# Hash attention and two feed-forward layers: the weight conversions and the sums of layer two rank 100 instructions later

## The chip, the cores and the metric

The kernel runs on one core of a Trainium2 chip. The metric is the device time of one execution in microseconds; the time shown is the median of three runs. TensorE (PE) multiplies matrices and loads weights (PEld) beside that; VectorE (DVE), ScalarE (ACT) and GpSimd (POOL) work element by element; SyncE (SP) issues nearly all DMAs, in the order of its queue.

## The reference

```python
# attention: q, k, v of 2 batches x 8 heads x 768 positions x 64
q_bits = einsum(q, proj) > 0;  k_bits = einsum(k, proj) > 0      # 6 bits each
mask   = q_bucket[..., :, None] == k_bucket[..., None, :]
scores = where(mask, q @ k.T / 8, -1e9)
attn   = exp(scores - max) / (sum + 1e-9);   out = attn @ v
# layer one: x is 1536 x 512, w_in 512 x 2048, w_out 2048 x 512
h = maximum(x @ w_in, 0);                    x = (h * h) @ w_out
# layer two: the same sizes
h = x @ w_in;  g = maximum(h, 0) + alpha * minimum(h, 0);  y = g @ w_out
```

The arrays of both layers come as float64, laid out by the host; the kernel gets them as their bits, two 32-bit words for each number.

## The kernel before, in words

The 1536 tokens are four chunks of 384. The attention of the first chunk runs alone (`attention_first`, L529). Then follow four passes of layer one, one for each chunk (`feed_forward`, L813); beside the passes of chunks 0 to 2 the attention of the next chunk is woven in, as a list of small steps (`attention_beside`, L572). The pass of the last chunk turns the result for layer two. Layer two takes two chunks at a time (`wide_hidden`, L989, and `whole_project`, L1075); its first product runs by a scheme with seven products in place of eight, for which sums of weight blocks are made beforehand.

All products are made of two parts of each operand: a rounded high part and the rest, and three matmuls (high by high, high by low, low by high). For a block of 128 hidden rows `split` (L737) makes the high part on ACT (L713) and the rest on VectorE or POOL (L714); `hidden` (L742) runs 12 matmuls with it (L752 to L754), and `project` (L786) runs those of the second product (L793, L794, L797).

Converting weights. `load_bits` (L648) loads 128 x 512 numbers of 8 bytes into one of three buffers `wbits`. `to_f32` (L654) makes float32 of them: ACT scales the upper words into `we` (L661), VectorE keeps the sign in `wsg` (L663), merges the bits of the lower words (L664), and joins both (L669). `we` and `wsg` have one buffer each. Layer one's 32 blocks are converted in `fetch` (L726) during the pass of chunk 0, two blocks of hidden rows ahead of their use, and stored to DRAM (L735); later passes load them from there (L731). Layer two's 32 blocks are converted during the passes of chunks 1 and 2: 16 of the second matrix in `ahead` (L672, stored at L676), 16 of the first in `sums_ahead` (L682), where VectorE then makes four sums of each pair of blocks (L697 to L700) and SP stores the results (L702, L703). These steps are spread over the passes from 1.0 to 2.9 by a list with marks:

```python
conversion = Background(steps, [(1.0, 0), (NCH - 1.1, len(steps))])
```

The attention beside: for each pair of heads and block of 128 queries, `scores` (L420) runs four matmuls (L426), VectorE takes the row maximum `low` (L434), and ACT the exponential `sm` (L435); `p_t` (L442) transposes it on TensorE (L451), and VectorE (L458) or ACT (L456) copies it to `pt`; `av` (L472) multiplies by the values. Hash bits (L254, L258), matches (L276, L302) and reciprocals of the sums (L483 to L488) come between.

The order on the engines. The program is traced instruction by instruction, and each gets a rank, its place in the trace. When the program is built, a scheduler goes through a model of the engines: an engine that is free takes, of its instructions that are ready, the one of lowest rank. The order that results is fixed for each engine and queue, and on the chip every engine works through its list in order. `tc.high_priority(offset=n)` takes n off the ranks of the instructions traced inside it. Before the change one place uses it: in the passes, maximum, exponential and copies of the transposes rank 100 ahead of their place.

```python
def urgent(self):
    return tc.high_priority(offset=URGENT if self.c else 0)
```

Of the kernel before, what the change touches and what calls it, by code (L numbers as in the profile page):

```python
# [13 lines left out]
ALU = mybir.AluOpType  # L14
# [9 lines left out]
EVICT = ("aavaav", "avavav", "vvavva", "vvavva")  # L24

LEAD = 0.88

URGENT = 100

# [2 lines left out]
def kernel(  # L32
# [20 lines left out]
    nc = tc.nc  # L53
# [518 lines left out]
    def attention_beside():  # L572


        pairs = [Pair(c, j) for c in range(1, NCH) for j in range(NPAIR)]
        steps, ends = [], []

        def begin():
            if (1, 0) not in raw:
                load_pair(1, 0)  # L580

        def turn(pr, u):
            for a in range(2):
                steps.append(lambda a=a: pr.p_t(*divmod(u, NTB), a))

        def values(pr, part):
            steps.append(lambda: pr.av(part))

        def finish(pr):
            steps.append(pr.finish)  # L590
            if pr.j == NPAIR - 1:
                ends.append(len(steps))

        steps += [begin] + pairs[0].prepare()
        last = 2 * NTB - 1
        for n, pr in enumerate(pairs):
            old = pairs[n - 1] if n else None
            prep = pairs[n + 1].prepare() if n + 1 < len(pairs) else []
            for u in range(2 * NTB):
                steps.append(lambda pr=pr, u=u: pr.scores(*divmod(u, NTB)))  # L600
                if prep and u != 1:
                    steps.append(prep.pop(0))
                if u == 0 and old:
                    turn(old, last)
                    steps.append(old.recip)
                    values(old, 0)
                if u == 1 and old:
                    values(old, 1)
                    values(old, 2)
                if u:  # L610
                    turn(pr, u - 1)
                if u == 4 and prep:
                    steps.append(prep.pop(0))
                if u == (3 if old and old.j == NPAIR - 1 else last) and old:
                    finish(old)
            assert not prep
        turn(pr, last)
        steps.append(pr.recip)
        for part in range(3):
            values(pr, part)  # L620
        finish(pr)
        return steps, ends
# [25 lines left out]
    def load_bits(u):  # L648
        l, f, o = u
        t = state["wide"].tile([P, DM, 2], U32, tag="wide", name="wbits")  # L650
        nc.sync.dma_start(out=t.rearrange("p n b -> p (n b)"), in_=(WO if o else WI)[l][f].bitcast(U32))
        w_bits[u] = t

    def to_f32(u, w=None):  # L654


        if u not in w_bits:
            load_bits(u)
        t = w_bits.pop(u)
        e = state["conv"].tile([P, DM], F32, tag="we", name="we")  # L660
        nc.scalar.activation(e, t[:, :, 1].bitcast(F32), AF.Copy, scale=2.0 ** -112)  # L661
        s = state["conv"].tile([P, DM], U32, tag="wsg", name="wsg")
        nc.vector.tensor_scalar(s, t[:, :, 1], 0x80000000, None, ALU.bitwise_and)  # L663
        nc.vector.scalar_tensor_tensor(s, t[:, :, 0], 29, s, ALU.logical_shift_right, ALU.bitwise_or)  # L664
        w = e if w is None else w
        eu, su = e.bitcast(U32), s
        if len(w.shape) == 3:
            eu, su = [a.rearrange("p (a n) -> p a n", a=2) for a in (eu, su)]
        nc.vector.scalar_tensor_tensor(w.bitcast(U32), eu, 3, su, ALU.logical_shift_left, ALU.bitwise_or)  # L669
        return w  # L670

    def ahead(u):  # L672

        w = to_f32(u)
        w_d[u] = dram.tile([P, DM], F32, tag="w%d_%d_%d" % u, name="w%d_%d_%d" % u)
        nc.sync.dma_start(out=w_d[u], in_=w)  # L676
# [5 lines left out]
    def sums_ahead(f, second):  # L682

        u = (1, f + NF * second, 0)
        if u not in w_bits:
            load_bits(u)
        w = w_bits[u].rearrange("p n b -> p (n b)").bitcast(F32).rearrange("p (a n) -> p a n", n=HM)
        to_f32(u, w[:, 0:2])  # L690
        if not second:
            sums_of[f] = w
            return
        v = sums_of.pop(f)
        a11, a12, s1, s2 = [v[:, i] for i in range(4)]
        a21, a22, s3, s4 = [w[:, i] for i in range(4)]
        nc.vector.tensor_tensor(s1, a21, a22, ALU.add)  # L697
        nc.vector.tensor_tensor(s3, a11, a21, ALU.subtract)
        nc.vector.tensor_tensor(s2, s1, a11, ALU.subtract)
        nc.vector.tensor_tensor(s4, a12, s2, ALU.subtract)  # L700
        w_sum[f] = dram.tile([P, 7, HM], F32, tag=f"ws{f}", name=f"ws{f}")
        nc.sync.dma_start(out=w_sum[f][:, 0:4], in_=v)  # L702
        nc.sync.dma_start(out=w_sum[f][:, 4:7], in_=w[:, 1:4])  # L703
# [22 lines left out]
    def fetch(i):  # L726

        for u in units(i):
            w_f[u] = state_whole.tile([P, DM], F32, tag="wf", name="wf")
            if u in w_d:  # L730
                nc.sync.dma_start(out=w_f[u], in_=w_d[u])  # L731
            else:
                to_f32(u, w_f[u])
                w_d[u] = dram.tile([P, DM], F32, tag="w%d_%d_%d" % u, name="w%d_%d_%d" % u)
                nc.sync.dma_start(out=w_d[u], in_=w_f[u])  # L735
# [385 lines left out]
    steps, ends = attention_beside()  # L1121
    following = Background(steps, [(0.0, 0)] + [(c + LEAD, n) for c, n in enumerate(ends)])
    steps = []
    for f in range(NF):
        for k in range(2):
            u = (1, f + NF * k, 0)
            steps += [lambda u=u: load_bits(u), lambda f=f, k=k: sums_ahead(f, k)]
        for u in ((1, f, 1), (1, f + NF, 1)):
            steps += [lambda u=u: load_bits(u), lambda u=u: ahead(u)]
# [130 lines left out]
```

## Time and profile before

| | |
|---|---|
| median of 3 runs | 808.34 us (808.32 to 808.45) |
| the profiled execution | 807.02 us, its span 805.2 us |
| TensorE busy | 768.8 us (95%) |
| VectorE busy | 550.3 us (68%) |
| ScalarE busy | 510.8 us (63%) |
| GpSimd busy | 319.5 us (40%) |
| DMA, mean over the span | 178 GB/s |
| conversions on VectorE | 57 to 468 us after the start |
| layer two alone | from about 501 us |

The span runs from the first to the last instruction of the profiled execution. All times of rows are microseconds from the span's start, of that one execution. "Busy" counts the time in which an engine executes; a mark such as [1.08 <-DVE pt L458] behind an instruction says that its engine was idle for 1.08 us before it, and that the VectorE instruction of line 458 that wrote `pt` ended the wait. Line numbers are those of the kernel before.

### The profile page before, as it was taken

The page shows a single profiled execution, that of the slowest core. Times are in us where ns is not written, and L with a number is a line of the kernel's source. Part 1 is how long each engine was busy: PE and PEld are TensorE (multiplying, and loading weights), DVE is VectorE, ACT ScalarE, POOL GpSimd, SP SyncE. Part 2 cuts the span into 40 slices and gives each one's busy share as a digit, 9 for nine tenths or more (in the row PEclk, how much of TensorE's full clock was granted, in tenths as well). Part 3 has the DMA queues.
Part 4 walks back from the last instruction along what each step waited for, and adds up shares of the span by engine and source line. Part 5 has one row for each costly group of instructions (what it writes and reads, how often), then busy time and mean ns, then how long its engine had stood idle before and what let it go on. Part 6 is the DMA issues. An engine that isn't in the chain of part 4 may idle for free. (4 is left out here: it accounts for less than half of the span.)

```text
span 805.2 us, 12580 instructions
## 1 busy us (share of the span) xinstructions
PE 768.8 (95%) x4354; PEld 633.1 (79%) x4354; DVE 550.3 (68%) x878; ACT 510.8 (63%) x990; POOL 319.5 (40%) x231
## 2 busy tenths in 40 slices
PE   6899999899999899999999999999999999999998
PEld 4565777677877677677776769999998888999886
DVE  7679899897756857788987965664666732676111
ACT  7778778766755646565655556865777634787331
POOL 1002322233456555653332442002667444558440
PEclk9999999999999999999999999999999999999999
DMA  6866787877787696777775568351311226411222
GB/s 169 213 178 222 223 283 220 257 223 228 226 267 225 179 260 186 244 246 258 243 271 186 199 202 298 110 171 60 103 67 53 65 76 213 176 68 44 66 66 92
DMA packets 56708, 143.67 MB, mean 178 GB/s; under 512 B 7402, under 2 KB 11652, under 8 KB 56644
## 3 DMA queue, kind: packets, MB, share of 16 engines
q1 hardware_dynamic: 56644, 142.87, 57.2%
q8 instruction: 34, 0.56, 0.3%
q14 instruction: 30, 0.25, 0.1%
HBM read 96.62 MB, written 25.47 MB: 152 GB/s over the span
## 5 line engine op out<-in xcount | busy, mean ns | idle before, releaser
L714 POOL TENSOR_TENSOR wl<-wf,wh 128x512 fp32r<-128x512 f32 x64 | 92.4, 1449 | 86.7 <-ACT wh L713 72.1
L985 POOL TENSOR_TENSOR wp<-wraw,wp 128x1024 fp32r<-128x1024 f32 (+1 forms) x32 | 68.2, 2135 | 115.5 <-ACT wp L982 102.6
L435 ACT ACTIVATE sm<-s,low 128x768 f32<-128x768 f32 x84 | 75.6, 899 | 54.9 <-DVE low L434 54.8
L713 ACT ACTIVATE wh<-wf 128x512 fp32r<-128x512 f32 x128 | 79.2, 628 | 42.7 <-PE h L753 19.8
L434 DVE TENSOR_REDUCE low<-s 128x1 f32<-128x768 f32 x84 | 80.1, 953 | 29.1 <-PE s L426 28.4
L765 POOL TENSOR_TENSOR gl<-g,gh 128x384 fp32r<-128x384 f32 x48 | 54.2, 1129 | 114.9 <-ACT g L762 51.2
L451 PE MATMUL m<-ident,sm 128*128 128x128 f32 x525 | 84.0, 276 | 7.6 <-DVE pt L458 3.2
L451 PEld LDWEIGHTS m<-ident,sm 128*128 128x128 f32 x525 | 63.8, 140 | 28.8 <-DVE pt L458 4.0
L426 PE MATMUL s<-k,q 128*128 128x384 f32 x336 | 77.7, 352 | 7.4 <-ACT sm L435 7.4
L1072 POOL TENSOR_TENSOR gp<-g,gp 128x768 fp32r<-128x768 f32 x32 | 62.2, 1949 | 51.4 <-ACT gp L1069 51.3
L752 PE MATMUL h<-xh,wh 128*128 128x384 f32 x212 | 77.7, 366 | 0.9 <-ACT r L759 0.5
L1082 PE MATMUL b<-wp,gp 128*128 128x512 f32 x192 | 75.0, 391 | 0.0
L950 PE MATMUL b<-xph,wp 128*128 128x384 f32 x224 | 74.8, 334 | 0.0
L948 PE MATMUL b<-xph,wp 128*128 128x384 f32 x224 | 74.8, 334 | 0.0
L949 PE MATMUL b<-xpl,wp 128*128 128x384 f32 x224 | 74.8, 334 | 0.0
L1083 PE MATMUL b<-wp,gp 128*128 128x512 f32 x192 | 74.8, 389 | 0.0
L426 PEld LDWEIGHTS s<-k,q 128*128 128x128 f32 x336 | 57.6, 190 | 20.7 <-ACT sm L435 13.5
L754 PE MATMUL h<-xh,wl 128*128 128x384 f32 x212 | 72.2, 341 | 1.6 <-POOL wl L714 1.6
L753 PE MATMUL h<-xl,wh 128*128 128x384 f32 x212 | 71.8, 339 | 0.1
L458 DVE COPY pt<-m 128x384 f32<-128x384 f32 x96 | 52.5, 550 | 23.3 <-PE m L451 23.3
L1066 DVE TENSOR_TENSOR wp<-wp 128x512 fp32r<-128x512 f32 x28 | 25.7, 928 | 62.2 <-ACT wp L1063 62.2
L793 PE MATMUL acc<-wh,gh 128*128 128x512 f32 x144 | 64.6, 449 | 0.0
(181 smaller groups left out, 1830.3 us busy)
## 6 DMA issues: line engine op xcount, KB each, us to landing
wf<-w SPq DMA_DIRECT2D x96, 256.0 KB, 4.0
wbits<-in_w_in_dram SPq DMA_DIRECT2D x32, 512.0 KB, 3.8
wbits<-in_w_out_dram SPq DMA_DIRECT2D x32, 512.0 KB, 4.7
wraw<-ws SPq DMA_DIRECT2D x16, 896.0 KB, 7.0
q<-q SPq DMA_DIRECT2D x48, 192.0 KB, 3.9
w<-wf SPq DMA_DIRECT2D x32, 256.0 KB, 2.3
wp<-w SPq DMA_DIRECT2D x32, 256.0 KB, 2.6
k<-kh SPq DMA_DIRECT2D x14, 384.0 KB, 6.6
```

What stands on the lines that cost most here:

```text
L426: self.pe(nc.tensor.matmul(ps[:, a, 0:HALF], self.q[:, h, i, qs], self.k[:, h, i, ks], start=i == 0, stop=i == 1))
L434: low_ins = nc.vector.tensor_reduce(low, ps[:, 0:2, 0:HALF], AX.XY, ALU.max, negate=True)
L435: sm_ins = nc.scalar.activation(sm.rearrange("p (a n) -> p a n", a=2), ps[:, 0:2, 0:HALF], AF.Exp, bias=low, accum_out=self.sums[:, i:i + 1],)
L451: self.pe(nc.tensor.transpose(ps[:, i * P:(i + 1) * P], pp[:, b * P:(b + 1) * P], ident))
L713: nc.scalar.activation(hi, w, AF.Copy)
L714: engine.tensor_tensor(lo, w, f32(hi), ALU.subtract)
L752: nc.tensor.matmul(hp, wih[:, ks], xh[:, kk, :], start=first, stop=False)
L948: nc.tensor.matmul(ps, w[0][:, ms], gh, start=first, stop=False, skip_group_check=True)
L949: nc.tensor.matmul(ps, w[0][:, ms], gl, start=False, stop=False, skip_group_check=True)
L950: nc.tensor.matmul(ps, w[1][:, ms], gh, start=False, stop=last, skip_group_check=True)
L1082: nc.tensor.matmul(a, g[:, 0, b], w[:, 0], start=f == 0, stop=False)
L1083: nc.tensor.matmul(a, g[:, 0, b], w[:, 1], start=False, stop=False)
```

## The change

A constant `LATER = 100` is added. The four instructions of a conversion move into a function of their own, `converted`, which is called under `tc.high_priority(offset=-LATER)`, so that their ranks rise by 100. The four sums of a pair of layer-two blocks are put under the same. Loads, stores, splits and all else keep their ranks; no instruction is added or removed.

```diff
+LATER = 100
...
     def to_f32(u, w=None):
...
         if u not in w_bits:
             load_bits(u)
         t = w_bits.pop(u)
+        with tc.high_priority(offset=-LATER):
+            return converted(t, w)
+
+    def converted(t, w):
+
         e = state["conv"].tile([P, DM], F32, tag="we", name="we")
         nc.scalar.activation(e, t[:, :, 1].bitcast(F32), AF.Copy, scale=2.0 ** -112)
         s = state["conv"].tile([P, DM], U32, tag="wsg", name="wsg")
...
     def sums_ahead(f, second):
...
         a11, a12, s1, s2 = [v[:, i] for i in range(4)]
         a21, a22, s3, s4 = [w[:, i] for i in range(4)]
-        nc.vector.tensor_tensor(s1, a21, a22, ALU.add)
-        nc.vector.tensor_tensor(s3, a11, a21, ALU.subtract)
-        nc.vector.tensor_tensor(s2, s1, a11, ALU.subtract)
-        nc.vector.tensor_tensor(s4, a12, s2, ALU.subtract)
+        with tc.high_priority(offset=-LATER):
+            nc.vector.tensor_tensor(s1, a21, a22, ALU.add)
+            nc.vector.tensor_tensor(s3, a11, a21, ALU.subtract)
+            nc.vector.tensor_tensor(s2, s1, a11, ALU.subtract)
+            nc.vector.tensor_tensor(s4, a12, s2, ALU.subtract)
```

## Rows read from the trace of the kernel before

**Rows 1.** Stretches: us; busy us (x instructions) of each engine; granted clock, DMA share, GB/s.
```profile
core 0: us, PE busy (x) PEld busy (x) DVE busy (x) ACT busy (x) POOL busy (x), PEclk, DMA share, GB/s
57.00:223.00 166.00, 159.63 (x991) 120.91 (x992) 146.58 (x243) 126.21 (x260) 53.21 (x44) 1.00 0.77 234
223.00:351.00 128.00, 119.88 (x693) 91.17 (x693) 87.44 (x133) 73.38 (x148) 72.65 (x62) 1.00 0.75 226
348.00:352.00 4.00, 2.53 (x8) 2.17 (x9) 3.90 (x8) 3.22 (x7) 1.97 (x3) 0.78 0.73 267
351.00:481.00 130.00, 124.92 (x689) 96.41 (x688) 109.57 (x175) 77.60 (x156) 50.12 (x41) 0.99 0.69 228
352.00:356.00 4.00, 4.00 (x22) 3.74 (x21) 3.40 (x5) 1.51 (x3) 1.85 (x2) 0.79 0.81 250
501.00:805.00 304.00, 300.58 (x1566) 277.17 (x1564) 154.68 (x235) 179.88 (x323) 130.91 (x66) 1.00 0.30 96
```

**Rows 2.** Timeline of TensorE: start, us, instruction, count [idle before <-releaser].
```profile
249.42 0.55 PE L451 MATMUL m<-ident,sm 128*128 128x128 f32 x3 [1.08 <-DVE pt L458]
...
279.87 0.49 PE L276 MATMUL s<-bits,code 128*128 128x192 bf16 x4 [2.23 <-ACT sm L435]
...
349.47 0.44 PE L426 MATMUL s<-k,q 128*128 128x384 f32 x1 [1.88 <-ACT sm L435]
...
434.36 0.27 PE L486 MATMUL m<-ident,rin 128*6 128x128 f32 x1 [1.84 <-DVE pt L458]
...
459.31 0.45 PE L426 MATMUL s<-k,q 128*128 128x384 f32 x1 [1.19 <-ACT sm L435]
```

**Rows 3.** Timeline of VectorE ahead of three of these waits.
```profile
246.38 1.66 DVE L664 SCALAR_TENSOR_TENSOR wsg<-wbits,wsg 128x512 uint32<-128x512 uint32 x1
247.96 0.94 DVE L434 TENSOR_REDUCE low<-s 128x1 f32<-128x768 f32 x1
...
275.73 1.23 DVE L698 TENSOR_TENSOR wbits<-wbits 128x256 f32<-128x256 f32 x1
...
277.85 0.94 DVE L434 TENSOR_REDUCE low<-s 128x1 f32<-128x768 f32 x1
...
346.02 1.50 DVE L698 TENSOR_TENSOR wbits<-wbits 128x256 f32<-128x256 f32 x1
347.45 0.95 DVE L434 TENSOR_REDUCE low<-s 128x1 f32<-128x768 f32 x1
```

**Rows 4.** Timeline of POOL beside the first of them.
```profile
246.02 3.14 POOL L714 TENSOR_TENSOR wl<-wf,wh 128x512 fp32r<-128x512 f32 x2
```

**Rows 5.** Two lines of VectorE: count, duration in ns min/median/max, first and last start.
```profile
L664 DVE SCALAR_TENSOR_TENSOR wsg<-wbits,wsg x64: 669/693/1764, 57.6 to 464.6; 128x512 uint32<-128x512 uint32 x64
...
L483 DVE TENSOR_SCALAR rin<-sums x16: 160/172/1258, 23.4 to 463.1; 128x6 f32<-128x6 f32 x16
```

**Rows 6.** Groups of VectorE, 57 to 223 us: count, busy us, mean ns, idle before.
```profile
L664 DVE SCALAR_TENSOR_TENSOR wsg<-wbits,wsg 128x512 uint32<-128x512 uint32 x34 | 26.0, 764 | 0.7
L669 DVE SCALAR_TENSOR_TENSOR wf<-we,wsg 128x512 uint32<-128x512 uint32 x32 | 25.6, 800 | 1.9 <-DVE wsg L664 0.4 <-POOL wl L714 0.3 <-ACT we L661 0.3
L663 DVE TENSOR_SCALAR wsg<-wbits 128x512 uint32<-128x512 uint32 x34 | 18.3, 539 | 3.6 <-DMA wbits<-in_w_in_dram 2.7 <-DMA wbits<-in_w_out_dram 0.6
```

**Rows 7.** Timeline: splits of two blocks on VectorE, first matmuls of those blocks.
```profile
147.44 0.68 DVE L714 TENSOR_TENSOR wl<-wf,wh 128x512 fp32r<-128x512 f32 x1
...
150.44 0.42 PE L752 MATMUL h<-xh,wh 128*128 128x384 f32 x1
...
156.78 0.68 DVE L714 TENSOR_TENSOR wl<-wf,wh 128x512 fp32r<-128x512 f32 x1
...
159.87 0.34 PE L752 MATMUL h<-xh,wh 128*128 128x384 f32 x1
```

**Rows 8.** Timeline of VectorE and TensorE around a late load of bits.
```profile
145.03 0.43 DVE L663 TENSOR_SCALAR wsg<-wbits 128x512 uint32<-128x512 uint32 x1 [2.73 <-DMA wbits<-in_w_in_dram]
...
146.71 0.33 PE L451 MATMUL m<-ident,sm 128*128 128x128 f32 x1 [1.19 <-DVE pt L458]
```

**Rows 9.** Waits of SP's queue, 57 to 481 us: us in all, times, longest.
```profile
SPq L735 <- DVE wf L669: 36.3, 24, 3.6
```

## The prediction

> **What bounds the kernel now.** I read the stages first, as busy time of each engine in five stretches. From 57 to 481 us, where the first feed-forward layer runs beside the attention of the next chunks, TensorE is busy 159.63 of 166 us, 119.88 of 128 and 124.92 of 130; from 501 to 805 us, where the second layer runs alone, 300.58 of 304 [rows 1]. TensorE is the bound everywhere. The conversions all lie between 57 and 481 us, so all that a new order of them can win is the idle time of TensorE there: 6.4 + 8.1 + 5.1 = 19.6 us, 2.4% of the span. What it can lose has no such lid.
>
> Next I asked what ended TensorE's longest waits. Five of those after 240 us have the same history: 1.08, 2.23, 1.88, 1.84 and 1.19 us, together 8.2 us [rows 2]. TensorE waits for ACT's exponential or for VectorE's copy of the transposes; these wait for VectorE, and VectorE is in the middle of a conversion or a sum. Three are shown: at 246.38 us the second conversion step takes 1.66 us and the row maximum starts only at 247.96; at 275.73 a sum takes 1.23 us in a run of them and the maximum follows at 277.85; at 346.02 a sum takes 1.50 us and the maximum follows at 347.45 [rows 3]. After the third of these the granted clock is 0.78 and 0.79 in the two stretches from 348 to 356 us [rows 1], so TensorE ran a part of them at 1.2 instead of 2.4 GHz. At full clock those 8 us would have held 4 x 0.22 + 4 x 0.21 = 1.7 us more of work. So the conversions stand in front of 8.2 + 1.7 = 9.9 us of the 19.6.
>
> Why are they that long? The second step (L664) takes 693 ns in the median and up to 1764 ns [rows 5]. The long ones lie beside work of POOL: a split runs there from 246.02 us [rows 4].
>
> **The change, part by part.** No instruction is added or removed. One ACT step and three VectorE steps of each of 64 conversions, and the 32 sums, get a rank 100 later; the loads of the bits, the stores of the results and the splits that follow keep theirs. A hundred is about one block of 128 hidden rows: in the first chunk's pass the engines execute 991 + 243 + 260 + 44 instructions for 16 blocks, 96 for each [rows 1].
>
> *Against the attention's maximum, exponential and copies:* these already rank 100 ahead of their place, so a conversion ran before them either because it was traced over 100 instructions earlier, or because they weren't ready when the scheduler placed it. Only the first kind moves. The trace doesn't show ranks, so I bound the gain: nothing, if all five waits are of the second kind, and 9.9 us, if all of it goes. I take a third, 3.3 us: the rows with a sum in front are a run of several sums with the same old rank, where a maximum can slip in between, while the long L664 is one instruction that nothing interrupts, and that is the commoner shape.
>
> *Against the splits, squares, hash bits and reciprocals, which have their plain rank:* here the conversions give way where both are ready. In the pass of the first chunk that is a cost, since the conversion of a block is followed by its split and its matmuls. Conversions take 26.0 + 25.6 + 18.3 = 69.9 us of VectorE's 146.58 in that pass [rows 6, 1], so VectorE is crowded. The slack is small: the split of one block starts at 147.44 and takes 0.68 us, and its matmuls start at 150.44; of the next, 156.78 plus 0.68 and 159.87 [rows 7]. That leaves 2.3 and 2.4 us. If each of the three VectorE steps of a conversion lets one ready instruction of about 0.68 us go ahead, a conversion comes 2.0 us later and the two of a block 4.1 us later, 1.7 us past the slack. Over the eight blocks of the pass's second half this is 14 us at the far end. At the near end it is nothing, because the matmuls of the attention cover it. I take 0.5 us: mostly only one of the three steps will meet something ready, which is 0.68 us and inside the slack.
>
> *DMAs and queues:* a store of a converted block issues on SP's queue, in its order, and SP waits 36.3 us in all for the last step of conversions [rows 9]. A conversion that comes later holds up what is queued behind that store: loads of queries and keys, and the next load of bits, which also needs one of three buffers that conversions free. What that costs can be seen once: at 145.03 us VectorE has idled 2.73 us for late bits, with a copy of transposes queued behind, and TensorE then idles 1.19 us [rows 8]. I count it with the rival below and at zero here, since the loads are traced a block ahead. In the passes of the second and third chunk the results of the conversions are read only in the second layer, and a delay by 100 instructions hides behind the last pass, 481 to 501 us and on. If that cover were gone, the second layer would start late by the whole delay; I see no way to that.
>
> *Where a removed stall goes:* a maximum that comes before the sums releases the exponential sooner; then the next things late are the splits on POOL and the sums themselves, which nobody waits for until the second layer.
>
> The sum is 3.3 - 0.5 = 2.8 us gained. The profiled execution took 807.02 us (span 805.2), so it would be 804.2; the median of the runs is 1.3 us above the profiled one, which makes **805.5 us**.
>
> **A rule that speaks against the gain.** On the rows alone, a long conversion step is long because POOL is at work, and the same stretch falls on other VectorE instructions: a tiny addition (L483), 172 ns in the median, has taken 1258 [rows 5]. The Trainium skill ("SBUF — State Buffer", section "SBUF: two separate sides") says that VectorE and GpSimd lock a shared pair of ports for a whole instruction, and that the other one waits. By that rule a conversion that moves away from a POOL instruction leaves the wait to the next VectorE instruction in line, and the gain would be zero; the trace agrees as far as the long L483.
>
> **Rivals.** *No change.* The stretch passes on to whatever stands beside POOL, and VectorE in the passes of the second and third chunk is busy only 87.44 of 128 and 109.57 of 130 us [rows 1], so the scheduler has free room there and starts a conversion as soon as its bits are in, whatever its rank. For it: the three waits where the step in front is simply long [rows 3]. Against it: in the first pass VectorE has work for 88% of the time, and some swaps must happen there. It gives 808.3 us.
>
> *Slower.* The place is the first chunk's pass, in its chain of bits, conversion, split, matmuls. A conversion that loses its place delays its split, keeps its buffer and so the next load, and VectorE, which works in order, then stands waiting for bits with a copy for the attention behind it, as at 145.03 us [rows 8]. It decides once two conversions of a block are late by more than the 2.3 us of slack [rows 7]. With four such blocks at 1.7 us each it is 6.8 us, or 815 us; a single wait like those above that also pulls the clock down costs 1.7 us more. For it: the slack is that thin, and VectorE that full. Against it: TensorE was busy 159.63 of 166 us in this pass although the conversions were late already, because there are matmuls of the attention to fill with.
>
> That the change doesn't do what it says would be a rank that the order never shows; that is part of the case of no change.
>
> **How the numbers follow.** I give the forecast (sums and conversions step out of the way of the attention, at a small cost in the first pass) 44%, no change 24%, slower 32%. A measurement of this kernel tells about 0.2%, 1.6 us, from no change; I read faster as below 806.7, slower as above 810. The likeliest case's own range is 798.4 (the whole 9.9 us, nothing lost) to 806.7. The range from 799 to 814 takes in nearly all of that, the case of no change, and the slower one up to about three late blocks and a fall of the clock (808.3 + 3 x 1.7 = 813.4); the far end of the cost, 808.3 + 14 = 822, is left out with the last bit of gain, about 2 in 10 together.
>
> **What would show it right or wrong.** Right: TensorE busy by 2 to 4 us more from 223 to 481 us for the same length, the maxima no longer behind runs of sums, the granted clock at 1.00 from 348 to 356 us, and matmuls of the first pass at most 1 us later behind their splits. No change: the same waits, with the same long steps, at other places. Slower: more idle time of VectorE for bits and of TensorE from 100 to 215 us, SP waiting longer for the last conversion step, and the second layer's start moved from 501 us by the loss. The prediction is wrong if TensorE's idle time between 57 and 481 us grows past 21 us, or falls without the sums having moved.

## The result

The changed kernel takes 814.23 us (median of 4 runs, 813.23 to 816.12), the kernel before 808.39 beside it: 1.0068 of the time before, 95% interval 1.0041 to 1.0094. It is slower by 0.7%; the forecast was 805.5, the range ended at 814.0.

Two slow executions, one of e13 (1513.76 us) and one of e16 (2270.99 us), are left out of the ratios and clocks below, though not of the medians of their rows.

The profiled execution of the changed kernel took 813.23 us. Its lines are numbered 2 to 8 higher: the maximum is L436 and the exponential L437, a conversion L668 (ACT), L670, L671 and L676 (VectorE), a sum L705 to L708, a split L721 and L722, the first matmul of a block L760. The page begins:

```profile
span 811.4 us, 12571 instructions
...
PE 771.7 (95%) x4354; PEld 635.6 (78%) x4354; DVE 561.1 (69%) x878; ACT 510.2 (63%) x990; POOL 320.2 (39%) x231
```

The span grew by 6.2 us. TensorE is busy 771.7 us after 768.8 for the same 4354 matmuls, 2.9 us more, and idle 811.4 - 771.7 = 39.7 us after 36.4, 3.3 us more. So half of the loss is waiting, and the other half is the same work taking longer. The stretches of the changed kernel, in the columns of [rows 1], show both:

```profile
57.00:223.00 166.00, 156.18 (x958) 116.69 (x958) 147.79 (x234) 121.24 (x252) 48.38 (x41) 1.00 0.75 228
223.00:351.00 128.00, 122.97 (x708) 94.73 (x707) 88.74 (x133) 74.94 (x151) 74.06 (x62) 0.97 0.74 224
351.00:481.00 130.00, 122.10 (x681) 94.22 (x680) 110.88 (x178) 76.31 (x155) 49.60 (x39) 0.99 0.68 221
...
284.00:288.00 4.00, 3.53 (x21) 3.02 (x21) 1.18 (x2) 1.95 (x5) 2.51 (x2) 0.72 0.99 313
288.00:292.00 4.00, 4.00 (x25) 3.59 (x25) 2.83 (x5) 2.71 (x6) 0.59 (x1) 0.85 0.94 235
324.00:328.00 4.00, 2.59 (x13) 2.46 (x14) 3.93 (x9) 3.63 (x9) 1.57 (x2) 0.84 0.32 128
328.00:332.00 4.00, 4.00 (x17) 3.43 (x16) 3.65 (x6) 2.07 (x5) 4.00 (x3) 0.73 0.70 231
...
436.00:440.00 4.00, 1.88 (x11) 1.30 (x10) 4.00 (x11) 2.11 (x6) 0.00 (x0) 0.92 0.76 260
440.00:444.00 4.00, 4.00 (x14) 1.89 (x14) 2.50 (x6) 1.62 (x3) 2.47 (x2) 0.65 0.94 295
```

In the first pass TensorE now idles 9.8 us where it idled 6.4, in the next stretch 5.0 in place of 8.1 (the work arrives there later, so the stretches don't hold quite the same), in the third 7.9 in place of 5.1. The granted clock falls three times in place of once: the six short stretches lose 4 x (0.28 + 0.15 + 0.16 + 0.27 + 0.08 + 0.35) = 5.2 us of full clock, against 1.7 us of the one fall before [rows 1].

Where the time is lost shows when both kernels are measured to the same matmul, the first of layer one's second pass:

```profile
225.07 0.42 PE L752 MATMUL h<-xh,wh 128*128 128x384 f32 x1
57.00:225.07 168.07, 161.70 (x1003) 122.60 (x1004) 148.65 (x247) 126.75 (x262) 54.07 (x44) 1.00 0.77 235
...
231.14 0.35 PE L760 MATMUL h<-xh,wh 128*128 128x384 f32 x1
57.00:231.14 174.14, 163.65 (x1004) 122.26 (x1003) 155.62 (x247) 126.38 (x263) 52.30 (x44) 1.00 0.74 225
```

The first two lines are of the kernel before, the others of the changed one. To this matmul the changed kernel takes 6.1 us longer, with as many matmuls and at full clock: TensorE waits 174.14 - 163.65 = 10.5 us in place of 6.4 and is busy 2.0 us longer. From there to the end it takes 580.3 us, the kernel before 580.1. So the loss of this execution is made in the first pass, before the first fall of the clock; the two more falls behind it don't show in the time.

TensorE's idle time from 57 to 481 us is 22.7 us after 19.6, past the 21 us that the prediction named as a sign of being wrong. Long waits stand ahead of all three falls, those that end at 284.47, 325.41 and 439.53 us; in TensorE's timeline:

```profile
82.43 0.45 PE L760 MATMUL h<-xh,wh 128*128 128x384 f32 x1 [1.26 <-ACT u L480]
...
284.47 0.33 PE L278 MATMUL s<-bits,code 128*128 128x192 bf16 x2 [2.06 <-ACT sm L437]
...
325.41 0.45 PE L428 MATMUL s<-k,q 128*128 128x384 f32 x1 [2.27 <-ACT sm L437]
...
355.21 0.45 PE L428 MATMUL s<-k,q 128*128 128x384 f32 x1 [2.02 <-ACT sm L437]
...
439.53 0.37 PE L488 MATMUL m<-ident,rin 128*6 128x128 f32 x1 [2.12 <-DVE pt L460]
...
465.24 0.44 PE L428 MATMUL s<-k,q 128*128 128x384 f32 x1 [1.08 <-ACT sm L437]
```

Of the last five, four answer to waits of [rows 2]; the one at 325.41 us has no counterpart there, and the wait of 1.08 us at 249.42 us is gone. Ahead of the waits at 284.47 and 325.41 us VectorE still has sums in front of the maximum; at 322.34 us it is one sum, and the next comes only after the maximum (timeline of VectorE):

```profile
280.69 0.87 DVE L707 TENSOR_TENSOR wbits<-wbits 128x256 f32<-128x256 f32 x1
281.59 0.94 DVE L708 TENSOR_TENSOR wbits<-wbits 128x256 f32<-128x256 f32 x1
282.45 0.94 DVE L436 TENSOR_REDUCE low<-s 128x1 f32<-128x768 f32 x1
...
322.34 1.12 DVE L705 TENSOR_TENSOR wbits<-wbits 128x256 f32<-128x256 f32 x1
323.39 0.94 DVE L436 TENSOR_REDUCE low<-s 128x1 f32<-128x768 f32 x1
...
324.72 0.41 DVE L706 TENSOR_TENSOR wbits<-wbits 128x256 f32<-128x256 f32 x1
```

The first wait, at 82.43 us, is new in its size; before, layer one's first matmul stood so:

```profile
80.78 0.45 PE L752 MATMUL h<-xh,wh 128*128 128x384 f32 x1 [0.35 <-ACT u L478]
```

In the changed kernel, on ACT, a conversion of block 2 stands in front of the copy `u` of the last pair of the first chunk, and it waited for VectorE's long last step of the conversion before it (the timeline of VectorE, one row, and of ACT):

```profile
79.71 1.59 DVE L676 SCALAR_TENSOR_TENSOR wf<-we,wsg 128x512 uint32<-128x512 uint32 x1
...
81.33 0.67 ACT L668 ACTIVATE we<-wbits 128x512 f32<-128x512 f32 x1 [1.72 <-DVE wf L676]
81.91 0.47 ACT L480 ACTIVATE u<-h 128x384 f32<-128x384 f32 x1
```

A conversion whose rank was raised stands in front of a copy that is needed at once. That would fit a conversion that was ready first in the scheduler's model, so that ranks weren't asked; no run shows the model.

### The profile page after: what moved, and what is told of

Read it like the earlier page. It is cut to its first block, busy times and chain, and to the rows that moved or that the text cites. A ratio compares the mean times of both kernels' runs of the same rounds, so it can differ in the third digit from the quotient of the medians.

```text
span 811.4 us, 12571 instructions
## 1 busy us (share of the span) xinstructions
PE 771.7 (95%) x4354; PEld 635.6 (78%) x4354; DVE 561.1 (69%) x878; ACT 510.2 (63%) x990; POOL 320.2 (39%) x231
## 5 line engine op out<-in xcount | busy, mean ns | idle before, releaser
L722 POOL TENSOR_TENSOR wl<-wf,wh 128x512 fp32r<-128x512 f32 x64 | 92.1, 1442 | 79.1 <-ACT wh L721 67.3
L437 ACT ACTIVATE sm<-s,low 128x768 f32<-128x768 f32 x84 | 75.7, 901 | 60.3 <-DVE low L436 60.0
L721 ACT ACTIVATE wh<-wf 128x512 fp32r<-128x512 f32 x128 | 79.6, 628 | 44.4 <-PE acc L805 14.0
L436 DVE TENSOR_REDUCE low<-s 128x1 f32<-128x768 f32 x84 | 79.9, 951 | 27.7 <-PE s L428 27.2
L760 PE MATMUL h<-xh,wh 128*128 128x384 f32 x212 | 77.9, 368 | 1.9 <-ACT u L480 1.3
```

Source lines behind the costliest of these rows:

```text
L436: low_ins = nc.vector.tensor_reduce(low, ps[:, 0:2, 0:HALF], AX.XY, ALU.max, negate=True)
L722: engine.tensor_tensor(lo, w, f32(hi), ALU.subtract)
L760: nc.tensor.matmul(hp, wih[:, ks], xh[:, kk, :], start=first, stop=False)
```

## The experiments

Three theories stood at the start. **A:** layer one's conversions, in the first pass, make the loss; in a narrow form by the late start at 82.4 us alone, in a wide form by the lateness of every block. **B:** layer two's conversions and sums make it, in front of the attention. **C:** any new order is a new draw of the waits, and the order before was a good draw. In the diffs `-LATER if ... else 0` stands for the rank offset of a conversion.

| run | median us | against before, 95% interval | mean granted clock (before beside it) | rows moved, TensorE / VectorE |
|---|---|---|---|---|
| the change | 814.23 | 1.0068 (1.0041 to 1.0094) | 0.9938 | 77 / 151 |
| e1 layer two and sums | 809.27 | 1.0017 (1.0001 to 1.0033) | 0.9961 (0.9967) | 2 / 30 |
| e2 layer one | 815.75 | 1.0090 (1.0060 to 1.0120) | 0.9924 (0.9967) | 79 / 147 |
| e3 first four | 812.65 | 1.0058 (1.0040 to 1.0076) | 0.9920 (0.9967) | 67 / 134 |
| e4 all but the first four | 810.35 | 1.0033 (1.0016 to 1.0049) | 0.9965 (0.9967) | 29 / 71 |
| e5 start repaired | 814.51 | 1.0082 (1.0050 to 1.0114) | 0.9925 (0.9962) | 85 / 118 |
| e6 rank 10 | 813.00 | 1.0048 (1.0030 to 1.0066) | 0.9948 (0.9962) | 87 / 113 |
| e7 100 ahead | 817.97 | 1.0112 (1.0078 to 1.0146) | 0.9935 (0.9962) | 105 / 171 |
| e8 sums on POOL | 824.19 | 1.0189 (1.0161 to 1.0217) | 0.9902 (0.9962) | 10 / 32 |
| e9 block 5 | 810.57 | 1.0028 (1.0013 to 1.0044) | 0.9942 (0.9958) | 33 / 43 |
| e10 sums behind a maximum | 810.52 | 1.0014 (0.9996 to 1.0032) | 0.9972 (0.9958) | 18 / 76 |
| e11 control, 0.879 | 809.56 | 1.0015 (0.9992 to 1.0038) | 0.9965 (0.9958) | 13 / 21 |
| e12 control, 0.882 | 807.52 | 0.9986 (0.9971 to 1.0002) | 0.9987 (0.9958) | 46 / 48 |
| e13 second conversion | 813.22 | 1.0055 (1.0038 to 1.0071) | 0.9940 (0.9963) | 83 / 146 |
| e14 fourth conversion | 813.33 | 1.0064 (1.0042 to 1.0086) | 0.9943 (0.9963) | 69 / 135 |
| e15 all but the second | 822.12 | 1.0162 (1.0124 to 1.0200) | 0.9920 (0.9963) | 71 / 133 |
| e16 as e12 again | 807.78 | 0.9984 (0.9969 to 0.9999) | 0.9978 (0.9963) | 46 / 48 |

Each row is compared with runs of the kernel before on the same chip, whose medians were 807.94 (e1 to e4), 808.91 (e5 to e8), 809.11 (e9 to e12) and 808.84 us (e13 to e16). The clock is the mean over the runs of a row. The last column compares the lists that the scheduler wrote with those of the kernel before, which have 3048 rows on TensorE and 827 on VectorE (equal instructions in a run are one row): it counts the rows that a shortest line-by-line comparison finds new.

**Which part makes the loss.** Four kernels divide the change.

e1, layer two's conversions and the sums later:

```diff
-        with tc.high_priority(offset=-LATER):
+        with tc.high_priority(offset=-LATER if u[0] else 0):
             return converted(t, w)
```

> Only layer two's conversions and the sums rank 100 later; layer one's keep their place. Theory A (the loss is made by layer one's conversions in the pass of the first chunk, the rest only follows): within 1.6 us of before, 806.8 to 810.0. Theory B (the loss is made by layer two's conversions and sums in front of the attention in the passes of chunks 1 and 2): 812 to 815. Theory C (any new order is a new draw of the waits): anything from 802 to 815, with waits at places that the moved instructions don't explain.

Measured: 1.0017, at the edge of what can be told. The two waits behind sums are still there, with three sums in one run ahead of the first maximum and the fourth behind it (timelines of TensorE and of VectorE of e1):

```profile
280.50 0.48 PE L278 MATMUL s<-bits,code 128*128 128x192 bf16 x2 [2.92 <-ACT sm L437]
...
352.30 0.44 PE L428 MATMUL s<-k,q 128*128 128x384 f32 x1 [1.92 <-ACT sm L437]
```

```profile
275.39 1.04 DVE L705 TENSOR_TENSOR wbits<-wbits 128x256 f32<-128x256 f32 x1
276.36 1.23 DVE L706 TENSOR_TENSOR wbits<-wbits 128x256 f32<-128x256 f32 x1
277.52 1.04 DVE L707 TENSOR_TENSOR wbits<-wbits 128x256 f32<-128x256 f32 x1
278.48 0.94 DVE L436 TENSOR_REDUCE low<-s 128x1 f32<-128x768 f32 x1
...
279.82 0.41 DVE L708 TENSOR_TENSOR wbits<-wbits 128x256 f32<-128x256 f32 x1
```

The kernel before has the same order in both places: the maxima of [rows 3] at 277.85 and 347.45 us already stand between sums (timeline of VectorE before):

```profile
279.18 0.41 DVE L700 TENSOR_TENSOR wbits<-wbits 128x256 f32<-128x256 f32 x1
...
348.32 0.41 DVE L699 TENSOR_TENSOR wbits<-wbits 128x256 f32<-128x256 f32 x1
```

In the lists that the scheduler wrote, e1 differs from before in 2 rows of TensorE and 30 of VectorE: the rank seldom decides there. Theory B falls.

e2, layer one's conversions alone:

```diff
+        with tc.high_priority(offset=0 if u[0] else -LATER):
             return converted(t, w)
```

> Only layer one's 32 conversions rank 100 later; layer two's and the sums keep their place. Theory A: 812.5 to 815.5, the first pass starting about 1.6 us late as in the changed kernel. Theory B: 807 to 810. Theory C: anything from 802 to 815.

Measured: 1.0090, the whole loss. e2 moves 79 rows of TensorE, the change itself 77.

e3, the four conversions of blocks 0 and 1 alone, and e4, all but these four:

```diff
# e3
+        with tc.high_priority(offset=-LATER if u[0] == 0 and u[1] < 2 else 0):
             return converted(t, w)
# e4
+        with tc.high_priority(offset=0 if u[0] == 0 and u[1] < 2 else -LATER):
             return converted(t, w)
```

> Only the four conversions of the first two blocks rank 100 later, those that are made while the attention of the first chunk still runs. Theory A in its narrow form (the late start of the first pass is the cause): the first matmuls of layer one at 82.4 us and not at 80.8 us, and 810 to 815. Theory A in its wide form (the chain of all blocks): 808 to 810, as only the start is late by 1.6 us. Theory B: 807 to 809.

> The change without those four: all other conversions and the sums rank 100 later. Theory A, narrow: 806 to 810, as before. Theory A, wide: 812 to 815. Theory B: 812 to 815.

Measured: 1.0058 and 1.0033. The first four conversions alone lose most of what the change loses, and the others alone lose too. In e3 the runs lose (1 - 0.9920) x 813 = 6.5 us by the clock against (1 - 0.9967) x 808 = 2.7 beside it: by the clock 3.8 us more, beside the 4.7 by which the medians differ; how much of it fell into time that TensorE waited anyway isn't known.

**How the first ones act.** e5 repairs the late start of the changed kernel with one edge:

```diff
+                if u == (0, 2, 1):
+                    with tc.issue_after(state["awaited"].ins):
+                        to_f32(u, w_f[u])
```

> The changed kernel, with one edge more: ACT's step of the sixth conversion (block 2, second matrix) stands behind the copy u of the last pair of the first chunk, for which the first pass waits. Theory A, narrow (the late start, made by that conversion in front of u, is the cause): the wait before the first matmuls of layer one falls from 1.26 to under 0.5 us, they start by 81.5 us, and the time falls to 808 to 811. If the start comes earlier and the time stays at 813 to 815, the start is a symptom only (theory C, or the waits further on). Theory A, wide: 811 to 813.

Measured: 1.0082, no better than the change. The wait before the first matmuls of layer one is back at 0.35 us; they start at 81.83 us, 0.6 us earlier than in the changed kernel and still 1.05 us later than before (the profiled execution is e5's fastest, 809.70 us):

```profile
81.83 0.44 PE L766 MATMUL h<-xh,wh 128*128 128x384 f32 x1 [0.35 <-ACT u L480]
```

So e5 repairs a third of the delay, not all of it. What decides are e14 and e15 below, which lose 0.64 and 1.62% though their first matmuls start at 80.61 and 80.73 us, as before: a loss as large needs no late start. Theory A in its narrow form falls.

e6 sets the distance to 10, e7 turns the sign:

```diff
-LATER = 100
+LATER = 10      # e6; in e7 LATER = -100
```

> The changed kernel with 10 in place of 100. Theory A (a conversion loses ties to splits of the same block or the one before, which are traced only a few instructions later): the size hardly matters, 811 to 815. If the distance mattered (conversions stepping back by about a block): less than half of the loss, 808 to 810.5. Theory C: anything from 802 to 815.

> The other way round: conversions and sums rank 100 ahead of their place. If layer one's conversions are what the first pass waits for (theory A), ahead is no loss in the first pass, and the time is 806 to 810, unless the conversions now stand in front of the attention's maximum as equals: then up to 813. Theory C: anything from 802 to 815.

Measured: 1.0048 and 1.0112. Ten ranks do most of what a hundred do, so ties (two instructions ready together, of which the rank picks one) between instructions traced close together are enough, without a block's distance. Going ahead costs more than stepping back, but that doesn't show that lateness is harmless: in e7 layer one's first matmul comes later still, and the granted clock is 0.54 and 0.61 from 80 to 88 us, so its loss may have a cause of its own:

```profile
85.13 0.69 PE L760 MATMUL h<-xh,wh 128*128 128x384 f32 x1 [0.17 <-ACT u L480]
```

e9 moves a single block in the middle of the first pass:

```diff
+        with tc.high_priority(offset=-LATER if u[:2] == (0, 5) else 0):
             return converted(t, w)
```

> The kernel before; only the two conversions of block 5 of layer one rank 100 later, in the middle of the first pass. Theory A, wide (each late conversion costs in its chain): up to 1.7 us more for one block, 808.5 to 810.5. Theory C (a new order is a new draw, and the order before is a good one): a loss of 2 to 6 us from one swapped block, 810 to 815, with waits far behind that block.

Measured: 1.0028, 2.3 us, with an interval from 1.1 to 3.6 us. That holds both the 1.7 us that theory A allows one block and the low end of theory C, so this run doesn't decide between them.

e13 and e14 move one conversion each, the second of block 0 and the second of block 1; e15 moves all but the first of these two. (The first conversion of either block, alone, moves no row of TensorE's list.)

```diff
# e13; in e14 u == (0, 1, 1)
+        with tc.high_priority(offset=-LATER if u == (0, 0, 1) else 0):
             return converted(t, w)
# e15
+        with tc.high_priority(offset=0 if u == (0, 0, 1) else -LATER):
             return converted(t, w)
```

> The kernel before; one conversion alone, the second of block 0, ranks 100 later, so that the split of the first goes ahead of it on ACT and VectorE. If one tie at the start carries most of the loss of the first four: 811 to 814, with the first pass 1.5 to 2 us late and long waits further on. If the four act together: 808.5 to 810.5.

> The same with the second conversion of block 1 alone. If the first tie is the cause: within 1.6 us of before, 807.5 to 810.5. If any tie lost at the start costs as much: 811 to 814.

> The change with that one conversion left at its place. If the one tie is the cause of most: 809 to 811, as where all first four keep their place. If ties lost anywhere in the first pass cost as much: 812 to 815.

Measured: 1.0055, 1.0064 and 1.0162. The rank of one conversion costs about as much as the whole change, that of another one as much by itself, both together (e3) no more than either; and the change without the first is worse than with it. So these don't add up, and no single conversion is the cause. In e13 the first matmul of layer one starts at 83.37 us and the granted clock is 0.88 and 0.69 from 80 to 88 us. In e14 the start is undisturbed, and long waits come some 65 and 200 us later, the second longer than any of [rows 2]:

```profile
147.10 0.33 PE L453 MATMUL m<-ident,sm 128*128 128x128 f32 x1 [2.05 <-DVE pt L460]
...
284.75 0.50 PE L278 MATMUL s<-bits,code 128*128 128x192 bf16 x3 [4.00 <-ACT sm L437]
```

**Is any new order worse?** Two controls move the mark of the attention by a thousandth or two of a pass. That moves 13 and 46 rows of TensorE's list and 21 and 48 of VectorE's, where the change moves 77 and 151, and gives no conversion another offset:

```diff
-LEAD = 0.88
+LEAD = 0.879    # e11; in e12 and e16 0.882
```

> A control: the kernel before, with the attention's mark at 0.879 of a pass in place of 0.88, so that the ranks of the attention's steps move a little against the rest and nothing of the conversions is touched. Theory C: as far from before as the changed kernel, 3 to 7 us, most likely slower. Theories A and B: within 1.6 us, 807 to 810.

> The same control with 0.882. Theory C: 3 to 7 us from before, most likely slower. Theories A and B: within 1.6 us, 807 to 810.

> The control with the attention's mark at 0.882 of a pass once more, with five rounds. If its gain is real: 0.1 to 0.3% under the kernel before, the interval wholly under 1. If it was the spread of the runs: 0.999 to 1.001.

Measured: 1.0015, 0.9986 and, again, 0.9984. A new order of this small extent moves the time by some 0.15%. Theory C in its plain form, that any new order costs, falls: e12 and e16 (one kernel) move rather more rows than e9, which loses 0.28%, and cost nothing. All eleven kernels in which a rank of a layer-one conversion was changed (the change, e2 to e7, e9, e13 to e15) lose 0.3 to 1.6%; e1, e10 and the controls, in which none was, stay within 0.2% (e8, below, is a case of its own). But no control is as large as the change, and, e8 aside, the kernels that lose 0.48% or more move 67 to 105 rows of TensorE's list, the others 46 at most. That a reordering as large would be harmless without the conversions is not shown.

The place points to the conversions all the same. At the first matmul of the second pass the profiled executions are late against before, and at the end of the span, by: the change 6.1 and 6.2 us, e2 8.3 and 8.7, e3 3.3 and 4.0, e6 7.5 and 7.2, e9 3.2 and 3.3, e13 4.8 and 4.5, e15 11.4 and 15.4, e7 8.5 and 12.0, e5 1.9 and 2.7, e14 3.1 and 5.7. e1 is late by nothing there, the controls by 0.9 to 2.6. In e4, which keeps the first four conversions at their place, it is 0.8 of 5.7. These are single executions of kernels whose runs differ by some us.

The second control is faster than the kernel before by 0.16%, in its second series with an interval that just excludes 1; that is all the gain found here.

**What stands in front of a maximum.** e8 moves the sums to POOL, e10 puts each run of sums behind the next maximum:

```diff
# e8, the same for all four
-        nc.vector.tensor_tensor(s1, a21, a22, ALU.add)
+        nc.gpsimd.tensor_tensor(s1, a21, a22, ALU.add)
# e10, in scores(), behind the exponential
+            if self.c and pending:
+                with tc.issue_after(low_ins.ins):
+                    pending.pop(0)()
```

> The kernel before, with the 32 sums on POOL in place of VectorE. If sums in front of the maximum cost what the waits at 279.87 and 349.47 us show (2.23 + 1.88 us, and 1.7 us for the clock behind the second), those waits go and the time falls by 3 to 6 us, to 802 to 805. If such waits pass on to whatever stands beside POOL next (POOL has 32 instructions more), the time stays within 1.6 us of before, or rises to 812 where a split on POOL comes late.

> The kernel before; the four sums of each pair of blocks are traced behind the next maximum of the attention, with an edge that keeps them there. If a run of sums in front of a maximum costs what the trace of before shows (2.23 and 1.88 us, and a fall of the clock), these two waits go and the time falls by 2 to 5 us, to 803 to 806. If VectorE only meets the same stretch elsewhere, 807 to 812.

Measured: e8 1.0189, the slowest kernel of all; e10 1.0014, not distinguishable from before. In e8 POOL has 32 instructions more, and TensorE waits longer for the exponential of scores (9.8 us, before 4.4 from 223 to 481 us), and once 3.0 us for the high part of a split; two of its waits from 223 us on (waited for: us in all, times, longest):

```profile
PE s L426 <- ACT sm L435: 9.8, 5, 3.8
...
PE h L752 <- ACT wh L713: 3.0, 1, 3.0
```

In e10 the sums are out of the way of the first maximum, and its wait remains: in front of it VectorE now has another instruction, lengthened to 1.36 us from the 0.55 that most of its kind take, beside POOL. At the second wait the edit doesn't do what was meant: kept behind one maximum, a sum of 1.50 us stands close in front of the next (timelines of VectorE, of POOL and of TensorE of e10):

```profile
279.77 1.36 DVE L522 TENSOR_TENSOR u<-u,rb 128x384 f32<-128x384 f32 x1
281.06 0.94 DVE L436 TENSOR_REDUCE low<-s 128x1 f32<-128x768 f32 x1
...
353.86 1.50 DVE L706 TENSOR_TENSOR wbits<-wbits 128x256 f32<-128x256 f32 x1
355.28 0.68 DVE L669 SCALAR_TENSOR_TENSOR wsg<-wbits,wsg 128x512 uint32<-128x512 uint32 x1
355.88 0.94 DVE L436 TENSOR_REDUCE low<-s 128x1 f32<-128x768 f32 x1
```

```profile
279.38 1.34 POOL L773 TENSOR_TENSOR gl<-g,gh 128x384 fp32r<-128x384 f32 x1
```

```profile
283.08 0.33 PE L278 MATMUL s<-bits,code 128*128 128x192 bf16 x2 [2.12 <-ACT sm L437]
...
357.91 0.45 PE L428 MATMUL s<-k,q 128*128 128x384 f32 x1 [2.48 <-ACT sm L437]
```

At the first maximum the stretch goes to the VectorE instruction that now meets POOL's. The rule of the Trainium skill that the prediction set against its own gain ("SBUF — State Buffer", section "SBUF: two separate sides": one of the two engines has the shared ports for a whole instruction, the other waits) would have it so, and these rows agree with it: the 1.36 us end 0.41 us after POOL's instruction. Not every instruction is lengthened: the maximum keeps its time throughout the kernel before, also at 277.85 us, beside an instruction of POOL that starts at 277.72 us and takes 1.05 (ns, min/median/max):

```profile
L434 DVE TENSOR_REDUCE low<-s x84: 939/955/960, 12.3 to 460.8; 128x1 f32<-128x768 f32 x84
```

**What stays open.** Shown is that the loss comes with layer one's conversions and not with layer two's (e2, e1), that most of it is made in the first pass in the change, e2, e3 and e13, that the rank of one of them is enough (e13, e14), and that it needs neither a late start nor a block's distance. Theory A in its wide form, a price for every late block, doesn't fit e3, for which it had 808 to 810 us. Not shown is whether it matters that they are conversions, or only that they move much of the order: no control is as large as the change. Not shown either is by which steps the moved conversions lengthen the first pass. The conversions share one buffer each for `we` and `wsg`, so that a moved one moves all that follow, with the loads of bits behind them, while the controls start from the attention's marks; that would fit, but no run isolates it.

## Why the prediction was wrong

- *The bound.* TensorE is the bound, and the loss is its idle time and longer busy time. That held.
- *The gain of 3.3 us is the step that failed,* "I take a third" of the 9.9 us. e1 has this part alone and gains nothing (1.0017). The waits of 2.23 and 1.88 us [rows 2] are 2.92 and 1.92 there; those of 1.84 and 1.19 us shrink to 0.90 and 0.87, but others come, and TensorE idles 20.8 us from 57 to 481 us in place of 19.6. The prediction hoped for sums "where a maximum can slip in between". In the kernel before the maxima had slipped in already: one after the third of four sums, one after the second (the rows at 279.18 and 348.32 us above). So the maximum, 100 ranks ahead of its place, had what a rank could give it. That it wasn't ready sooner in the scheduler's model, the second kind of case that the prediction named, fits this; no run shows the model.
- *The cost of 0.5 us in the first pass* was too small by far: layer one's conversions alone cost 0.9%, 7 us (e2). The working was wrong too. Slack of 2.3 us and what goes past it [rows 7] assumed that a block's lateness is paid as TensorE's idle time at that block. In the changed kernel blocks are late by up to 9 us (block 5 starts at 121.95 in place of 112.88 us, rows below), TensorE fills with the attention, and to the same matmul (231.14 us) it idles 4.1 us more. With 2.0 us of longer busy time that makes the 6.1 us that this pass costs, where the prediction had 0.5; by which steps stays open.

```profile
112.88 0.33 PE L752 MATMUL h<-xh,wh 128*128 128x384 f32 x1
...
121.95 0.33 PE L760 MATMUL h<-xh,wh 128*128 128x384 f32 x1
```

- *The clock.* That a wait pulls the clock down and costs 1.7 us more was in the text, but only as a line of the slower rival. The two more falls, 5.2 - 1.7 = 3.5 us of clock, don't explain the loss of the profiled execution: 2.0 of the 2.9 us of longer busy time were there at full clock, before the first fall, and what follows takes 0.2 us longer in all.
- *The rival "slower"* had the place and nearly the time (815 us), and not the mechanism; that the time is near is luck. Late bits were to hold VectorE up; it waits for them 1.0 us in all from 57 to 228 us of the changed kernel, against 2.7 + 0.6 before [rows 6]:

```profile
DVE wsg L670 <- DMA wbits<-in_w_out_dram: 1.0, 1, 1.0
```

- *The rival "no change"* is what holds for layer two's part: the rank moves almost nothing there (e1), and at one of the two maxima the stretch passed on (e10). The working of the rule there went too far in one point: the stretch doesn't pass to the next instruction whatever it is, since the maximum isn't lengthened.
- *The range* ended at 814 where the time was 814.2: it took three late blocks at most and left out the far end of a cost whose price rested on a slack, not on a row with such a loss. Its sum, 808.3 + 3 x 1.7 = 813.4, is said to hold three late blocks and a fall of the clock; these are four terms of 1.7 us, 815.1, past the range's own end.

## What to carry to other kernels

A rank decides only between instructions that are ready together in the scheduler's model; before expecting a gain from one, look for a row in which the instruction to be helped was ready and stood behind. A maximum that already stands between two sums has nothing left to gain. In a kernel in which TensorE is 95% busy, a rank need not be a local edit: price it by undoing it for a part, starting with the first instructions it touches, since one conversion there cost as much as all. Before laying a loss on the instructions moved, make a control that moves as many rows. A wait of TensorE of some 2 us can take the clock down with it; whether that costs time is asked by comparing the time between the same two matmuls, and here two more falls didn't show in it.

## What the hardware showed that was not expected

Waits of TensorE of about 2 us come with or without a fall of the clock: in the changed kernel behind 2.06, 2.27 and 2.12 us and not behind 2.02 us, before behind 1.88 us and not behind 2.23 us [rows 2]. Each fall costs about 1.7 us of full clock, 4 x (0.22 + 0.21) before and 4 x (0.28 + 0.15) at 284 us in the changed kernel. Over the runs of one kernel the clock varies: of e5 the runs took 809.7 us at a mean clock of 0.995 and 817.3 at 0.987, by this price some two and six falls, an estimate.
